# Second layer's first product from seven half-size products, with the first layer's side work on a written-out plan

## The chip, the cores and the metric

One core of a Trainium2 chip runs the whole program. The metric is the device time in microseconds (us) of one execution; lower is better. TensorE multiplies, VectorE (DVE), ScalarE (ACT) and GpSimd (POOL) do everything elementwise, and SyncE (SP) issues nearly all DMAs.

## The reference

```python
def _attn_ref(q, k, v):            # 4 x 8 heads, 576 tokens, 64 wide, float32
    ...
    scores = scale * np.matmul(q_rot, k_rot.transpose(0, 1, 3, 2))
    attn = softmax(scores)
    return np.matmul(attn, v)

def _moe_ref(x, w_in, w_out):      # first layer: x 2304 x 512, w_in 512 x 2048, w_out 2048 x 512
    h = np.maximum(x @ w_in, 0.0)
    return h * h @ w_out

def _moe2_ref(x, w_in, w_out, alpha):   # second layer, same sizes
    h = x @ w_in
    g = np.maximum(h, 0.0) + alpha * np.minimum(h, 0.0)
    return g @ w_out
```

Attention, then the first layer on its output, then the second layer. The weights arrive as float64 and are converted on the chip.

## The kernel before

**Precision.** Every float32 operand of the two layers is split into a high part, rounded to the format that TensorE takes at full rate, and a low part, the rest. A product is three matmuls: high by high, high by low, low by high. So every operand needs a copy to the high part (ACT) and a subtraction for the low part (DVE).

**Units.** The 2304 tokens are NB = 6 blocks of W = 384. A *unit* (layer, b, z, i) is one step of TensorE: with z = 0 it makes rows i of the hidden layer for block b (12 matmuls of 128 x 384: four parts of the 512-long sum, three matmuls each), with z = 1 it adds hidden rows i to the block's output (12 matmuls of 128 x 384 in the first layer, 9 of 128 x 512 in the second). There are 16 of each per block. Blocks 0 and 1 of the first layer are interleaved and overlap with the end of attention; from block 2 on the order is block by block, 16 units of z = 0 and then 16 of z = 1. `products` issues a unit's matmuls.

**What goes around a unit.** PE, DVE, ACT and POOL run in exactly the order in which the code is written (a manual schedule); SP's order is set by a planner. At step t, after the matmuls of unit t, the code issues `low_g` for unit t + 2 (the low part `gl` of a hidden tile, on DVE), `high_g` for unit t + 3 (the high part `gh`, on ACT), `finish` for unit t - 1, and then the *jobs* of step t. `finish` of a z = 0 unit takes the sum out of PSUM: in the first layer a Relu on ACT (L575) and a square, on ACT for even i (L581) and on POOL for odd i (L583); in the second a Relu on ACT, alpha times the negative part on DVE (L578) and their sum on POOL (L579).

**Jobs.** While the first layer's blocks 2 to 5 run, the second layer's 32 weight tiles (128 x 512 each) are loaded and converted, one every EVERY2 = 2.9 steps. One conversion is a load (three steps ahead), L384, L385 (`convert`) and L390 (`mask`) on DVE, L394 (`grow`) on ACT, L399 and L400 (`sign`) on DVE, then L405 on ACT and L406 on DVE (`join`), and a DMA that keeps the result in HBM. Other jobs prepare the next block's x: a product on POOL (L510, first layer only), the high part on ACT (L520) and the low part on DVE (L526). During the first layer's last block, `hold` loads each kept weight tile into the slot that the first layer has just stopped using.

Of the kernel before, what the change touches and what calls it, by code (L numbers as in the profile page):

```python
# [22 lines left out]
P = 128  # L23
# [328 lines left out]
EVERY0, EVERY1, EVERY2 = 1.8, 1.8, 2.9  # L352


class Weights:
# [55 lines left out]
def moe(tc, xd, rd, mats, pbias, dram, al, out):  # L411
# [11 lines left out]
    with ExitStack() as mo:  # L423
# [4 lines left out]
        Xf = X.rearrange("p y c w -> p (y c w)")  # L428
        Xw = [Xf[:, 1024 * k:1024 * k + 1024].rearrange("p (y n) -> p y n", y=2) for k in range(6)]
# [7 lines left out]
        units += [(layer, b, z, i) for layer in range(2) for b in range(0 if layer else FIRST, NB)  # L437
                  for z in range(2) for i in range(FC)]
# [4 lines left out]
        def slot(z, i):  # L443
            if z and OUT0 <= i < OUT0 + OUTX:
                return Xw[4 + i - OUT0]
            return late[("held0" if i < HELD0 else "held1") if z == 0 else ("out0" if i < OUT0 else "out1")].tile([P, 2, 512], F32R, name="w")

        def place(layer, z, i):
            if layer == 0:
                ws[0, z, i] = slot(z, i)  # L450
                return ws[0, z, i]
            return Xw[3]

        def done_with(wc, *j):
            if j[0]:
# [5 lines left out]
        def hold(z, i):  # L461
            w = slot(z, i)
            nc.sync.dma_start(out=w.bitcast(F32), in_=kept[1, z, i])
            ws[1, z, i] = w
# [4 lines left out]
        def hidden(layer, b, i):  # L469

            if first(layer, b):
# [5 lines left out]
            return gt[k][:, c0:c0 + W]  # L477

# [16 lines left out]
        def load_x(layer, b, c):  # L495
            c0 = b * W
            k = next(xbuf)
            xr, r = XT[:, k, 0], XT[:, k, 1]
            if layer == 0:
                nc.sync.dma_start(out=xr, in_=xd[:, c, c0:c0 + W])  # L500
                for j in range(2):
                    nc.sync.dma_start(out=r[64 * j:64 * j + 64], in_=rd[c, j:j + 1, c0:c0 + W].to_broadcast([D, W]))
            else:
                nc.sync.dma_start(out=xr, in_=x2[:, c, c0:c0 + W])
            xin[layer, b, c] = xr, r
# [22 lines left out]
        def products(u):  # L528
            layer, b, z, i = units[u]
            wh, wl = ws[layer, z, i][:, 0], ws[layer, z, i][:, 1]  # L530
# [9 lines left out]
            if i == 0:  # L540
                accs[layer, b] = [ps_h.tile([P, 512], F32, name="ph") if (layer, b) == (0, FIRST - 1) else
                                  late["ps_y"].tile([P, 512], F32, name=f"py{e}") for e in range(KC if layer == 0 else W // P)]
# [25 lines left out]
        def finish(u):  # L568

            layer, b, z, i = units[u]  # L570
            c0 = b * W
            if z == 0:
# [3 lines left out]
                if layer == 1:  # L576
                    mn = XT[:, u % 2, 1]
                    V.tensor_scalar(mn, ph, 0.0, al[:, i:i + 1], ALU.min, ALU.mult)  # L578
                    G.tensor_tensor(out=g, in0=g, in1=mn, op=ALU.add)  # L579
                elif i % 2 == 0 or first(layer, b):  # L580
                    A.activation(out=g, in_=g, func=AF.Square)  # L581
                else:
                    G.tensor_tensor(out=g, in0=g, in1=g, op=ALU.mult)  # L583
# [39 lines left out]
        for k in range(2 * FC):  # L623
            job(NF + EVERY2 * k, conv[1], 1, k // FC, k % FC)
        for c in range(KC):
            for layer in range(2):
                for b in range(0 if layer else FIRST, NB):
                    prior = (layer, b - 1) if b else (layer - 1, NB - 1)
                    job((NF - 16 if prior == (0, FIRST - 1) else at_unit[prior + (1, 0)]) + 4 * c,
                        ((-2, load_x), (0, join_x), (2, high_x), (3, low_x)), layer, b, c)  # L630
# [13 lines left out]
        late["held0"] = pool("held0", HELD0, side="right")  # L644
# [6 lines left out]
        for t in range(-STEPS_AHEAD - 1, NU + 1):  # L651
            if t == EARLY:
                late.update(held1=pool("held1", FC - HELD0), sp=pool("sp", 3), out0=pool("out0", OUT0),
                            g0=pool("g0", FC // 2), ps_y=pool("ps_y", 1, space=PSUM))
                gfirst = mo.enter_context(ExitStack())
                late["g1"] = gfirst.enter_context(tc.tile_pool(name="g1", bufs=FC // 2))
            if 0 <= t < NU:
                products(t)
# [3 lines left out]
            unfinished += [t - 1] if 0 <= t - 1 < NU else []  # L662
            if "g0" in late:
                while unfinished:
                    finish(unfinished.pop(0))
            if t == at_unit[0, FIRST - 1, 1, FC // 2 - 1]:
                gfirst.close()
                late["out1"] = pool("out1", FC - OUT0 - OUTX)
            for d, stage, j in sorted(jobs.get(t, []), key=lambda x: x[0]):
                stage(*j)  # L670
            if 0 <= t < NU:
                layer, b, z, i = units[t]
                if (layer, b) == (0, NB - 1):
                    hold(z, i)
            if t < EARLY:
                yield
# [56 lines left out]
```

## Time and profile before

| | |
|---|---|
| median of 3 runs | 1131.28 us (1129.35 to 1135.73) |
| the profiled execution | 1133.05 us, of which the span of instructions is 1131.3 us |
| TensorE busy | 1088.7 us (96%), 6480 matmuls |
| DVE, ACT, POOL busy | 600.3, 535.6, 312.3 us |
| mean granted TensorE clock | 0.989 of full speed (2.4 GHz) |
| HBM read and written | 80.26 MB and 31.01 MB |
| first layer, block 2 on | about 463 to 729.5 us |
| second layer | 729.5 us to the end |

Busy shares are means over stages with different limits: attention (to about 330 us), the first layer's blocks 0 and 1 (to about 463 us), its blocks 2 to 5, and the second layer. A matmul's own duration overlaps with the next one's, so the pace of TensorE is read from the distance between starts.

### The profile page before, as it was taken

The page shows a single profiled execution, that of the slowest core. Times are in us where ns is not written, and L with a number is a line of the kernel's source. Part 1 is how long each engine was busy: PE and PEld are TensorE (multiplying, and loading weights), DVE is VectorE, ACT ScalarE, POOL GpSimd, SP SyncE. Part 2 cuts the span into 40 slices and gives each one's busy share as a digit, 9 for nine tenths or more (in the row PEclk, how much of TensorE's full clock was granted, in tenths as well). Part 3 has the DMA queues.
Part 4 walks back from the last instruction along what each step waited for, and adds up shares of the span by engine and source line. Part 5 has one row for each costly group of instructions (what it writes and reads, how often), then busy time and mean ns, then how long its engine had stood idle before and what let it go on. Part 6 is the DMA issues. An engine that isn't in the chain of part 4 may idle for free.

```text
span 1131.3 us, 17531 instructions
## 1 busy us (share of the span) xinstructions
PE 1088.7 (96%) x6480; PEld 996.4 (88%) x6480; DVE 600.3 (53%) x1070; ACT 535.6 (47%) x1140; POOL 312.3 (28%) x304
## 2 busy tenths in 40 slices
PE   2899999999879999999999999999999999999997
PEld 1788887887769999999999999998989989898996
DVE  4665766766568989578596821233232323323232
ACT  1676776776548845455655533232232323223221
POOL 3665446663400000120211201050322305032230
PEclk9999999999979999999999999999999999999999
DMA  7768677675634433557566557800001020000101
GB/s 190 171 172 208 162 180 163 172 192 155 188 94 147 132 111 115 186 173 246 178 210 222 176 192 257 281 2 24 33 14 43 8 49 1 25 33 14 28 1 29
DMA packets 91733, 140.73 MB, mean 124 GB/s; under 512 B 21120, under 2 KB 62720, under 8 KB 91648
## 3 DMA queue, kind: packets, MB, share of 16 engines
q1 hardware_dynamic: 87856, 133.24, 41.1%
q10 hardware_dynamic: 3536, 6.24, 1.7%
q8 instruction: 51, 0.84, 0.3%
q14 instruction: 34, 0.28, 0.1%
q0 software_dynamic: 256, 0.13, 0.0%
HBM read 80.26 MB, written 31.01 MB: 98 GB/s over the span
## 4 chain that ended last, share of the span: by engine, by line
PE 87%; DMA 4%; DVE 3%; SPq 3%; ACT 1%; issue 1%; POOL 0%; ACTq 0%; DVEq 0%; POOLq 0%
PE py L553 32%; PE ph L535 12%; PE ph L536 12%; PE ph L537 12%; PE ps L264 7%; PE sc L196 6%; PE ps L218 4%; PE ph L553 2%; DMA vraw<-in_v_dram 2%; SPq L170 2%; PE ps L149 1%; DMA xt<-r 1%; DVE nm L199 1%; DMA kL<-nat 1%; PE ps L230 1%
## 5 line engine op out<-in xcount | busy, mean ns | idle before, releaser
L535 PE MATMUL ph<-xs,w 128*128 128x384 f32 x768 | 258.2, 336 | 3.2 <-ACT g L575 3.2
L536 PE MATMUL ph<-xs,w 128*128 128x384 f32 x768 | 257.7, 336 | 0.0
L537 PE MATMUL ph<-xs,w 128*128 128x384 f32 x768 | 257.5, 335 | 0.0
L490 DVE TENSOR_TENSOR gl<-g,gh 128x384 fp32r<-128x384 f32 x192 | 109.9, 574 | 174.9 <-PE py L553 123.1
L575 ACT ACTIVATE g<-ph 128x384 f32<-128x384 f32 x192 | 94.4, 492 | 210.0 <-PE ph L537 201.0
L579 POOL TENSOR_TENSOR g<-g,xt 128x384 f32<-128x384 f32 x96 | 101.9, 1062 | 295.5 <-DVE xt L578 295.5
L483 ACT ACTIVATE gh<-g 128x384 fp32r<-128x384 f32 x192 | 100.5, 524 | 160.6 <-PE py L553 145.2
L553 PE MATMUL py<-w,gh 128*128 128x512 f32 x504 | 155.3, 389 | 0.0
L199 DVE TENSOR_REDUCE nm<-sc 128x1 f32<-128x576 f32 x144 | 108.0, 750 | 84.2 <-PE sc L196 83.6
L535 PEld LDWEIGHTS ph<-xs,w 128*128 128x128 f32 x768 | 145.1, 189 | 4.6 <-ACT g L575 3.5
L553 PE MATMUL py<-gh,w 128*128 128x384 f32 x560 | 146.2, 335 | 0.0
L536 PEld LDWEIGHTS ph<-xs,w 128*128 128x128 f32 x768 | 145.1, 189 | 0.2
L537 PEld LDWEIGHTS ph<-xs,w 128*128 128x128 f32 x768 | 145.1, 189 | 0.0
L578 DVE TENSOR_SCALAR xt<-ph,al 128x384 f32<-128x384 f32 x96 | 59.3, 618 | 138.8 <-ACT g L575 132.2
L200 ACT ACTIVATE p<-sc,nm 128x576 f32<-128x576 f32 x144 | 107.0, 743 | 45.3 <-DVE nm L199 36.2
L553 PEld LDWEIGHTS py<-w,gh 128*128 128x128 f32 x504 | 94.5, 188 | 19.4
L553 PEld LDWEIGHTS py<-gh,w 128*128 128x128 f32 x560 | 101.8, 188 | 0.0
L553 PE MATMUL py<-w,gl 128*128 128x512 f32 x252 | 98.2, 389 | 0.0
L553 PE MATMUL py<-gl,w 128*128 128x384 f32 x280 | 94.0, 336 | 1.8 <-DVE gl L490 1.8
L196 PE MATMUL sc<-kH,qT 128*128 128x288 f32 x336 | 82.2, 331 | 12.6 <-DMA qT<-nat 11.3
L218 PE MATMUL ps<-ident,p 128*128 128x128 f32 x576 | 87.1, 279 | 0.2
L510 POOL TENSOR_TENSOR xt<-xt 128x384 f32<-128x384 f32 x24 | 27.5, 1149 | 216.6 <-DMA xt<-x 172.5
(102 smaller groups left out, 1617.7 us busy)
## 6 DMA issues: line engine op xcount, KB each, us to landing
w<-in_moe_w_in_dram SPq DMA_DIRECT2D x32, 512.0 KB
w<-in_moe_w_out_dram SPq DMA_DIRECT2D x32, 512.0 KB
wk<-xs SPq DMA_DIRECT2D x32, 512.0 KB
w<-wk SPq DMA_DIRECT2D x30, 512.0 KB
xt<-x SPq DMA_DIRECT2D x48, 192.0 KB
kH<-nat SPq DMA_DIRECT2D x62, 144.0 KB
qT<-nat SPq DMA_DIRECT2D x62, 144.0 KB
kL<-nat SPq DMA_DIRECT2D x62, 144.0 KB
```

The lines of the kernel that those rows point to most:

```text
L196: T.matmul(sc[:, hf, o0:o0 + w], lhsT=lhs, rhs=kx[:, c0:c0 + w], start=st and y == 0, stop=not st and y == len(prods) - 1 and o0 + w == SH)
L199: V.tensor_reduce(out=nm, in_=sc[:, :, 0:SH], axis=AX.XY, op=ALU.max, negate=True)
L200: A.activation(out=Pt[n, i][:, j * S:(j + 1) * S].rearrange("p (a b) -> p a b", a=2), in_=sc[:, :, 0:SH], func=AF.Exp, bias=nm, accum_out= ...
L218: T.transpose(u[:, c * P:(c + 1) * P], p[:, (S + 64) * j + c * P:(S + 64) * j + (c + 1) * P], ident)
L483: A.activation(out=hi, in_=hidden(layer, b, i), func=AF.Copy)
L490: V.tensor_tensor(out=lo, in0=hidden(layer, b, i), in1=gsp[u][0].bitcast(F32), op=ALU.subtract)
L535: T.matmul(ph[:, :W], lhsT=wh[:, cs], rhs=xh, start=(c == 0), stop=False)
L536: T.matmul(ph[:, :W], lhsT=wh[:, cs], rhs=xl, start=False, stop=False)
L537: T.matmul(ph[:, :W], lhsT=wl[:, cs], rhs=xh, start=False, stop=(c == KC - 1))
L553: T.matmul(acc, lhsT=x, rhs=y, start=(s0 and k == 0), stop=(s1 and k == 2))
L575: A.activation(out=g, in_=ph, func=AF.Relu)
L579: G.tensor_tensor(out=g, in0=g, in1=mn, op=ALU.add)
```

## The change

**Seven products instead of eight.** In the second layer the first product is made for two blocks at once. Weights and x are cut into halves (256 of 512 along the sum, hidden rows i and i + 8, and the two blocks), and the four half products of each pair come from seven products of sums and differences (Strassen's algorithm in Winograd's form). A unit is now (1, 2q, 0, i) for i = 0 to 7: seven products of 6 matmuls of 128 x 384, in the function `seven`. It is followed by the 32 z = 1 units of both blocks.

**What a unit of seven needs.** The x terms (7 per half, `T`, prepared by `prepare` during the z = 1 units before) stay in SBUF. The seven weight pieces of each i (256 KB each, `ws`) lie in HBM and pass through a ring of RING = 8 slots: after each product `refill` issues a DMA for the product eight later. Three PSUM banks A, B and C hold the products; what is in A or B must be copied out (`keep`, ACT) or added into a result (DVE) before the next product accumulates onto that bank. `leak` (DVE) and `join` (ACT, POOL) make the four hidden tiles.

**The first layer.** The weight pieces are made there: for each i, `sums` adds and subtracts the two converted halves: ten operations on POOL (two of 512 columns, eight of 256) with four copies on ACT between them, over six steps. Conversions stand at the steps in `TURNS` instead of every 2.9 steps, with the stages one step closer together, and use two load buffers of `st[0]` instead of four. All squares are on ACT.

```diff
-EVERY0, EVERY1, EVERY2 = 1.8, 1.8, 2.9
+EVERY0, EVERY1 = 1.8, 1.8
+SUMS_AT = 0, 0, 1, 2, 2, 2, 3, 3, 3, 4, 4, 4, 5, 5
+TURNS = {2: ((0, "in"), (3, "in"), (6, "out"), (10, "in"), (13, "in"), (16, "out"), (19, "out"), (21, "out"), (24, "in"), (27, "in")),
+         3: ((3, "in"), (6, "in"), (9, "out"), (12, "out"), (18, "out"), (21, "out"), (24, "in"), (27, "in")),
...
+RING = 8
+PRODUCTS = (0, "A", "11"), (1, "C", "21"), (2, "A", "T2"), (3, "B", "T1"), (4, "A", "T3"), (5, "B", "22"), (6, "A", "T4")
...
-                       ((-3, self.load), (0, self.convert), (1, self.mask), (2, self.grow), (3, self.sign), (4, self.join)))
+                       ((-3, self.load), (0, self.convert), (0, self.mask), (1, self.grow), (2, self.sign), (3, self.join)))
...
-        w64 = st[n // 2 % 2].tile([P, 512, 2], U32, name="w64", bufs=2)
+        w64 = st[0 if layer else n // 2 % 2].tile([P, 512, 2], U32, name="w64", bufs=2)
...
+        def sums(i, x):
+            u, v = (t.bitcast(F32) for t in late["pair"])
...
+            if x < 2:
+                t = (u, v)[x]
+                G.tensor_tensor(out=t[:, 0], in0=t[:, 0], in1=t[:, 1], op=ALU.add)
+                return
...
+            if x == 0:
+                G.tensor_tensor(out=f[k], in0=a, in1=b, op=op)
+            elif x == 1:
+                A.activation(out=o[:, 0], in_=f[k], func=AF.Copy)
+            else:
+                G.tensor_tensor(out=o[:, 1], in0=f[k], in1=o[:, 0].bitcast(F32), op=ALU.subtract)
+                nc.sync.dma_start(out=kept[i][:, p], in_=o.bitcast(F32))
...
+        def refill(n):
+            if n < 7 * HC * NG:
+                w = late["ring"][n % RING]
+                nc.sync.dma_start(out=w.bitcast(F32), in_=kept[n // 7 % HC][:, n % 7])
...
+        def seven(u):
...
+            def leak(n, ph):
+                s[n] = low()
+                V.tensor_scalar(s[n], ph, 0.0, al[:, i + HC * (n // 2):i + HC * (n // 2) + 1], ALU.min, ALU.mult)
+
+            def join(n, ph):
+                A.activation(out=h[n], in_=ph, func=AF.Relu)
+                G.tensor_tensor(out=h[n], in0=h[n], in1=s[n], op=ALU.add)
+
+            def keep(x, c):
+                s[x] = part()
+                A.activation(out=s[x], in_=bank[c], func=AF.Copy)
+
+            for p, c, x in PRODUCTS:
...
+                refill(k + p + RING)
+                if p == 0:
+                    keep("1", "A")
+                    if late.get("rest"):
+                        late.pop("rest")()
+                elif p == 1:
+                    V.tensor_tensor(out=h[0], in0=bank["C"], in1=s["1"], op=ALU.add)
+                    leak(0, h[0])
+                elif p == 2:
+                    keep("2", "A")
+                    join(0, h[0])
+                elif p == 3:
+                    keep("5", "B")
+                elif p == 4:
+                    V.tensor_tensor(out=h[3], in0=bank["A"], in1=s["5"], op=ALU.add)
+                    leak(3, h[3])
+                elif p == 5:
+                    V.tensor_tensor(out=h[1], in0=bank["B"], in1=s["2"], op=ALU.add)
+                    leak(1, h[1])
+                    join(3, h[3])
...
-                if layer == 1:
-                    mn = XT[:, u % 2, 1]
-                    V.tensor_scalar(mn, ph, 0.0, al[:, i:i + 1], ALU.min, ALU.mult)
-                    G.tensor_tensor(out=g, in0=g, in1=mn, op=ALU.add)
-                elif i % 2 == 0 or first(layer, b):
-                    A.activation(out=g, in_=g, func=AF.Square)
-                else:
-                    G.tensor_tensor(out=g, in0=g, in1=g, op=ALU.mult)
+                A.activation(out=g, in_=g, func=AF.Square)
...
-        for k in range(2 * FC):
-            job(NF + EVERY2 * k, conv[1], 1, k // FC, k % FC)
+                if z == 0 and i >= HC:
+                    for x, n in enumerate(SUMS_AT):
+                        job(at + 4 + n, ((0, sums),), i - HC, x)
```

POOL's order in the first layer, block 2 on, before: products of x (L510) and squares (L583) of the four blocks, nothing else.

```order
L510 TENSOR_TENSOR xt<-xt 128x384 x4
L583 TENSOR_TENSOR g<-g 128x384 x8
L510 TENSOR_TENSOR xt<-xt 128x384 x4
L583 TENSOR_TENSOR g<-g 128x384 x8
L510 TENSOR_TENSOR xt<-xt 128x384 x4
```

After, POOL's piece that falls into block 2's z = 1 units (`w_5594` and `w_5595` are the two converted halves, `q` a spare tile; L657 is the product of x, before L510):

```order
L657 TENSOR_TENSOR xt<-xt 128x384
L494 TENSOR_TENSOR w_5594<-w_5594 128x512
L494 TENSOR_TENSOR w_5595<-w_5595 128x512
L501 TENSOR_TENSOR w_5594<-w_5595 128x256
L505 TENSOR_TENSOR w_5595<-w_5594,w_5595 128x256
L501 TENSOR_TENSOR w_5594<-w_5594 128x256
L505 TENSOR_TENSOR q<-w_5594,q 128x256
L501 TENSOR_TENSOR w_5594<-w_5594,w_5595 128x256
L657 TENSOR_TENSOR xt<-xt 128x384
L505 TENSOR_TENSOR w_5595<-w_5594,w_5595 128x256
L501 TENSOR_TENSOR w_5594<-w_5594 128x256
L505 TENSOR_TENSOR q<-w_5594,q 128x256
```

Squares have left POOL; ten operations of the sums now lie between the products of x, in z = 1 units. DVE's order in the same units after the change (L640 is `gl`, before L490; L673 the low part of x; L393, L394, L399, L408, L409 and L415 are a conversion's L384, L385, L390, L399, L400 and L406 of before):

```order
L393 TENSOR_SCALAR m<-w_5896 128x512
L394 SCALAR_TENSOR_TENSOR m<-w_5896,m 128x512
L399 TENSOR_SCALAR w_5896<-w_5896 128x512
L640 TENSOR_TENSOR gl<-g,gh 128x384 x2
L408 SCALAR_TENSOR_TENSOR w_5896<-w_5896 128x512
L409 TENSOR_SCALAR w_5896<-w_5896 128x512
L393 TENSOR_SCALAR m<-w_5940 128x512
L394 SCALAR_TENSOR_TENSOR m<-w_5940,m 128x512
L399 TENSOR_SCALAR w_5940<-w_5940 128x512
L640 TENSOR_TENSOR gl<-g,gh 128x384
L415 SCALAR_TENSOR_TENSOR xs<-m,w_5896 128x512
L640 TENSOR_TENSOR gl<-g,gh 128x384
```

Conversions at steps 19 and 21 follow each other with two steps between, and TensorE's `gl` tiles stand behind them in the queue.

TensorE's order in one unit of seven after the first (`ph` are the PSUM banks, `xs` the ring), with what each row waits for:

```order
L599 MATMUL ph<-T,xs 128x384 [waits DMAHW3_49]
L599 MATMUL ph<-T,xs 128x384 x5
L599 MATMUL ph<-T,xs 128x384 [waits DMAHW4_49]
L599 MATMUL ph<-T,xs 128x384 x5
L599 MATMUL ph<-T,xs 128x384 [waits DMAHW5_49,Activation_49]
L599 MATMUL ph<-T,xs 128x384 x5
L599 MATMUL ph<-T,xs 128x384 [waits DMAHW6_49,DVE_49]
L599 MATMUL ph<-T,xs 128x384 x5
L599 MATMUL ph<-T,xs 128x384 [waits DMAHW7_49,Activation_49]
L599 MATMUL ph<-T,xs 128x384 x5
L599 MATMUL ph<-T,xs 128x384 [waits DMAHW0_49,Activation_49]
L599 MATMUL ph<-T,xs 128x384 x5
```

The seventh product (again 6 matmuls) waits for a DMA and DVE. A unit of z = 0 had 12 matmuls and one wait for a bank that had been free for three units; now every product of 6 waits for its refill, and the third to the seventh also for an engine that empties a bank.

## Rows read from the trace of the kernel before

**Rows 1.** Page, section 1: busy time, share of the span, instructions.
```profile
PE 1088.7 (96%) x6480; PEld 996.4 (88%) x6480; DVE 600.3 (53%) x1070; ACT 535.6 (47%) x1140; POOL 312.3 (28%) x304
```

**Rows 2.** Windows: stretch, length, busy us of each engine, clock, DMA share, GB/s.
```profile
430.00:463.00 33.00, 31.23 (x171) 30.89 (x170) 27.77 (x51) 15.45 (x30) 2.53 (x2) 0.95 0.50 162
496.50:529.80 33.30, 33.30 (x194) 33.30 (x193) 28.08 (x51) 16.80 (x31) 5.69 (x5) 1.00 0.67 218
696.20:729.50 33.30, 33.30 (x194) 33.30 (x193) 9.69 (x18) 9.45 (x19) 0.83 (x1) 1.00 0.86 272
729.50:762.80 33.30, 33.30 (x193) 33.30 (x193) 11.22 (x19) 9.04 (x19) 15.45 (x15) 1.00 0.16 53
```

**Rows 3.** Chain that ended last, in order of time: start us, us, what.
```profile
40.83 2.90 DMA kL<-nat
...
449.05 3.01 PE py L553 x11
452.07 2.86 PE ph L553 x12
...
563.09 33.28 PE py L553 x192
```

**Rows 4.** Timeline at a unit's end: start us, us, engine, line, operation.
```profile
731.41 0.33 PE L535 MATMUL ph<-xs,w 128*128 128x384 f32 x1
...
731.61 0.49 ACT L575 ACTIVATE g<-ph 128x384 f32<-128x384 f32 x1 [2.11 <-PE ph L537]
```

**Rows 5.** Timeline where TensorE waits for a bank to be emptied.
```profile
331.39 0.48 ACT L575 ACTIVATE g<-ph 128x384 f32<-128x384 f32 x1
...
331.92 0.29 PEld L535 LDWEIGHTS ph<-xs,w 128*128 128x128 f32 x1 [3.55 <-ACT g L575]
```

**Rows 6.** Lines by form, whole span: count, busy us, mean ns, idle before.
```profile
L579 POOL TENSOR_TENSOR g<-g,xt 128x384 f32<-128x384 f32 x96 | 101.9, 1062 | 295.5 <-DVE xt L578 295.5
L575 ACT ACTIVATE g<-ph 128x384 f32<-128x384 f32 x192 | 94.4, 492 | 210.0 <-PE ph L537 201.0 <-issue 8.6
L124 POOL TENSOR_TENSOR t<-kraw,tab 128x640 f32<-128x640 f32 x15 | 23.4, 1558 | 108.4 <-DMA kraw<-in_k_dram 86.0 <-DVE nm L199 14.3 <-DMA al<-in_moe_alpha_dram 7.5
L141 DVE TENSOR_TENSOR nat<-ps,nat 128x512 fp32r<-128x512 f32 x32 | 22.0, 687 | 2.0 <-ACT nat L140 1.8
L125 POOL TENSOR_TENSOR t<-kraw,tab 128x320 f32<-128x320 f32 x15 | 13.1, 872 | 0.0
L141 DVE TENSOR_TENSOR nat<-ps,nat 128x256 fp32r<-128x256 f32 x16 | 6.6, 415 | 0.0
```

**Rows 7.** Lines on DVE from 395 to 430 us, while POOL is idle.
```profile
L490 DVE TENSOR_TENSOR gl<-g,gh 128x384 fp32r<-128x384 f32 x16 | 8.8, 554 | 5.5 <-PE ph L553 3.0 <-PE py L553 2.5
L385 DVE SCALAR_TENSOR_TENSOR m<-w,m 128x512 f32<-128x512 uint32 x7 | 4.9, 694 | 0.2
L399 DVE SCALAR_TENSOR_TENSOR w<-w 128x512 uint32<-128x512 uint32 x6 | 4.1, 685 | 0.0
L390 DVE TENSOR_SCALAR w<-w 128x512 uint32<-128x512 uint32 x7 | 3.0, 430 | 0.2
L384 DVE TENSOR_SCALAR m<-w 128x512 uint32<-128x512 uint32 x7 | 3.0, 422 | 0.1
L406 DVE SCALAR_TENSOR_TENSOR w<-m,w 128x512 fp32r<-128x512 f32 x4 | 2.8, 694 | 0.1
L400 DVE TENSOR_SCALAR w<-w 128x512 uint32<-128x512 uint32 x6 | 2.6, 431 | 0.2
```

**Rows 8.** Timelines where DVE and POOL work at the same time.
```profile
99.77 0.69 DVE L141 TENSOR_TENSOR nat<-ps,nat 128x512 fp32r<-128x512 f32 x1
99.86 0.88 POOL L125 TENSOR_TENSOR t<-kraw,tab 128x320 f32<-128x320 f32 x1
...
507.87 1.55 POOL L510 TENSOR_TENSOR xt<-xt 128x384 f32<-128x384 f32 x1 [7.64 <-DMA xt<-x]
...
508.46 1.25 DVE L390 TENSOR_SCALAR w<-w 128x512 uint32<-128x512 uint32 x1
```

More of the change, by code (lines that the diff above doesn't have):

```diff
@@ L451, in place @@
                 return ws[0, z, i]
-            return Xw[3]
+            if z:
+                return Xw[3]
+            if "pair" not in late:
+                late["pair"] = [st[1].tile([P, 512, 2], U32, name="w64", bufs=2).rearrange("p n t -> p (n t)").bitcast(F32R)
+                                .rearrange("p (y n) -> p y n", y=2) for _ in range(2)]
+            return late["pair"][i // HC]
         def done_with(wc, *j):
-            if j[0]:
+            layer, z, i = j
+            if layer and z:
@@ L456, in done_with @@
                 kept[j] = dram.tile([P, 2, 512], F32, name="wk%d_%d_%d" % j)
                 nc.sync.dma_start(out=kept[j], in_=wc.bitcast(F32))
-        weights = Weights(tc, mats, pbias, place, done_with)
[L461 to L464, printed above, removed]
+            elif layer and i < HC:
+                kept[i] = dram.tile([P, 7, 2, 256], F32, name=f"ws{i}")
+                for k in range(2):
+                    nc.sync.dma_start(out=kept[i][:, k], in_=wc[:, :, 256 * k:256 * k + 256].bitcast(F32))
+            elif layer:
+                nc.sync.dma_start(out=kept[i - HC][:, 6], in_=wc[:, :, 256:512].bitcast(F32))
@@ L466, in first, with hold @@
+        def hold(i):
+            w = slot(1, i)
+            nc.sync.dma_start(out=w.bitcast(F32), in_=kept[1, 1, i])
+            ws[1, 1, i] = w
         def first(layer, b):
@@ new lines, in seven, with rest @@
+        def seven(u):
+            layer, b, z, i = units[u]
+            if "banks" not in late:
+                late["full"] = [ps_h.tile([P, 512], F32, name="ph") for _ in range(4)]
+                late["banks"] = [t[:, :W] for t in late["full"]]
+            bank = dict(zip("ABC", (late["banks"][i % 2], late["banks"][2], late["banks"][3])))
+            g = late["g0"].tile([P, XW], F32, name="g")
+            gt[i], gt[i + HC] = (g[:, :W], g[:, W:]), late["more"][2 * i:2 * i + 2]
+            h = [*gt[i], *gt[i + HC]]
+            part, low = (lambda x=x: next(late[x]) for x in ("part", "leak"))
+            k = 7 * (b // 2 * HC + i)
+            s = {}
+            def leak(n, ph):
[8 more added lines that the diff above has]
+            for p, c, x in PRODUCTS:
+                w = late["ring"][(k + p) % RING]
+                for kc in range(2):
+                    ws_, t = slice(128 * kc, 128 * kc + 128), late["T"][x, kc]
+                    first_ = p in (0, 1, 3)
+                    for n, (y0, y1) in enumerate(((0, 0), (0, 1), (1, 0))):
+                        T.matmul(bank[c], lhsT=w[:, y0, ws_], rhs=t[:, y1], start=first_ and kc == 0 and n == 0,
+                                 stop=kc == 1 and n == 2, skip_group_check=not first_)
+                refill(k + p + RING)
[18 more added lines that the diff above has]
+                    join(3, h[3])
+            def rest():
+                leak(2, bank["A"])
+                join(1, h[1])
+                join(2, bank["A"])
+            late["rest"] = rest
@@ L529, in products @@
             layer, b, z, i = units[u]
+            if layer and z == 0:
+                seven(u)
+                return
+            if late.get("rest"):
+                late.pop("rest")()
             wh, wl = ws[layer, z, i][:, 0], ws[layer, z, i][:, 1]
@@ L541, in products @@
                 accs[layer, b] = [ps_h.tile([P, 512], F32, name="ph") if (layer, b) == (0, FIRST - 1) else
-                                  late["ps_y"].tile([P, 512], F32, name=f"py{e}") for e in range(KC if layer == 0 else W // P)]
+                                  late["full"][1 + e] if layer and b % 2 and e < 2 else
+                                  late["ps_y"].tile([P, 512], F32, name=f"py{3 if layer and b % 2 else e}") for e in range(KC if layer == 0 else W // P)]
             gh, gl = gsp.pop(u)
@@ L571, in finish @@
             c0 = b * W
+            if layer and z == 0:
+                return
             if z == 0:
@@ L657, in moe @@
             if 0 <= t < NU:
+                if units[t][0] and units[t][2:] == (0, 0):
+                    finish(t - 1)
                 products(t)
@@ L661, in moe @@
                     split(t + d)
-            unfinished += [t - 1] if 0 <= t - 1 < NU else []
+            unfinished += [t - 1] if 0 <= t - 1 < NU and not (t < NU and units[t][0] and units[t][2:] == (0, 0)) else []
             if "g0" in late:
```

100 lines of the change are left out of this document (82 added, 18 removed).

## The prediction

> **What bounds the kernel now.** I read the page's busy times first: TensorE works 1088.7 of 1131.3 us [rows 1]. Then the windows by stage: from block 2 of the first layer to the end TensorE is busy for the whole of each stretch at full clock, while DVE, ACT and POOL have room [rows 2]. So after 463 us the time is TensorE's, and what the change gives or takes is read in its pace. One set of 16 units with 384-column matmuls takes 33.28 us for 192 of them [rows 3]: 173.3 ns a matmul, 2.08 us a unit. The second layer's z = 0 sets have that same length (729.5 to 762.8 us) [rows 2].
>
> The third view is the chain, where it leaves TensorE. The last such place is at 449 us: DVE is late with a `gl`, and TensorE's next 11 matmuls take 3.01 us and the next 12 take 2.86, where 1.91 and 2.08 are due [rows 3]. In 430 to 463 us TensorE is busy 31.23 of 33.00, DVE is at 27.77, and the granted clock averages 0.95 [rows 2]. A wait of 1.8 us thus cost about 1.8 us once more, at the lower clock level. A loaded DVE is what this kernel must fear.
>
> **What the seven products save.** Before: 6 blocks x 33.28 = 199.7 us. After: 3 pairs x 8 units x 42 matmuls x 0.1733 = 174.7 us. Columns, type and weight loads per matmul are as before, so I take the same pace. Term: **-25.0 us**, if TensorE never waits.
>
> **Hand-offs inside a unit of seven.** Each product lasts 6 x 0.1733 = 1.04 us. What it left in bank A or B must be out before the product after next begins, so the cover is one product. ACT starts 0.20 us after the first matmul of the next unit starts [rows 4] and takes 0.492 [rows 6]; TensorE goes on 0.05 us after ACT's end (331.39 + 0.48 to 331.92) [rows 5]. `keep` is thus through after 0.74 us, 0.30 before it is needed. The addition of `h[3]` on DVE reads one operand from PSUM and one from SBUF; the trace has 0.415 us for 256 columns and 0.687 for 512 [rows 6], so 0.55 for 384, and 0.80 in all: 0.24 to spare, less the 0.17 by which a weight load runs ahead. ACT's seven operations take some 3.5 us of a unit's 7.28, DVE's three additions and four leaks about 4, POOL's four additions 4 x 1.06 = 4.2 [rows 6]: all fit. I allow 0.06 us a unit: **+1.5 us**. Bounds: 0; and, if POOL stretched the addition of `h[3]` as it stretched L390 (0.43 to 1.25) [rows 7, 8], 0.5 us a unit, +12. I stay near zero, because the operation with the same kinds of operands ran 0.69 us under a POOL operation [rows 8], the 0.687 of its mean.
>
> **The first layer.** Here TensorE has no slack, so the change can only cost. ACT gains eight squares of about 0.5 us and some short copies per block of 66 us, and was about half busy (16.8 of 33.3 us in block 2's z = 1 set) [rows 2]. What counts is DVE and POOL together. L390 started while POOL's L510 ran and took 1.25 us instead of 0.43; it ended 0.29 us after L510, which itself took 1.55 [rows 7, 8] where 384 columns mean 1.06 [rows 6]. SBUF-to-SBUF work of the two runs one after the other. The Trainium skill (GPSIMD Engine Reference, "Specifications") says that GpSimd's SBUF interfaces are shared with VectorE, with contention for DVE operations in a 2-port mode or with two SBUF inputs. By that rule, which names no price, the extra POOL work costs something wherever such operations meet; by the row it is the full length of the operation, and my sum goes by the row.
>
> So I add up both engines' work in block 2's units 16 to 24 (z = 1), where TURNS starts conversions at steps 16, 19, 21 and 24 and `sums` lies on steps 17 to 22. A conversion's six DVE operations take 3.36 us: 1.55 at its step, 1.12 two steps on, 0.69 three steps on [rows 7]. In these nine steps stand four firsts, three seconds and four thirds: 12.3 us. Nine `gl` and two low parts of x at 0.554 [rows 7] add 6.1. POOL: by the line through 0.872 for 320 columns and 1.558 for 640 [rows 6] an operation of 256 takes 0.74 and one of 512 takes 1.28, so `sums` is 8.5 us; three products of x at 1.0 add 3. Together 29.9 us, in 9 x 2.08 = 18.7: 11.2 us behind. The same nine units before, with conversions at 17, 20 and 23, hold 10.1 + 6.1 + 3 = 19.2, no more than fits, and TensorE did not wait there [rows 2].
>
> The slack is that `gl` is issued two units ahead: 4.16 us, plus 0.17 (it enters with the second matmul), less 0.55 and 0.05: 3.7 us. Behind DVE in its queue stand the next `gl`; TensorE waits for those. If everything stood in one line the lag over the slack would be 7.5 us. It ends lower if POOL's operations fall behind rather than DVE's; in that case DVE alone (18.4 us in 18.7) is never late. The two alternate in rows 8, so I take about half, 4 us of waiting, and 2 us for the lower clock, by the 449 us place. Term: **+6 us**; bounds 0 and +11 (7.5 and half again). By the same count no other stretch of blocks 2 to 5 lags over 3 us, since there the sums lie in z = 0 units, where DVE owes TensorE nothing but a few operations. SP's stores change from 32 of 512 KB to 16 of those and 56 pieces of 256 KB, 16.8 to 23.1 MB over four blocks; with a DMA share of 0.67 [rows 2] I take them as hidden.
>
> **The step into the second layer.** During the first layer's last 16 units SP issues the 16 `hold` loads (8.4 MB), 8 refills (2.1) and x in four pieces (1.6): 12.1 MB in 33.3 us. Before, 272 GB/s stood at a DMA share of 0.86 [rows 2], so 316 at full share, and 12.1 MB need 38 us. ACT's high parts of the second x half stand ahead of `gh` in its queue, with three units of slack. I take **+1 us**, bounds 0 and +5.
>
> **Sum.** -25.0 + 1.5 + 6 + 1 = -16.5: the span goes from 1131.3 to 1114.8 us. The profiled execution took 1133.05 us, 1.75 around its span, and lies 1.8 above the median of 1131.28; the median should thus come to **1115 us**.
>
> **The rivals.**
>
> *No overload* (24 in 100): POOL's sums slip behind and DVE keeps its pace. For it: POOL has no deadline in those steps. Against: rows 8. Time: 1131.3 - 25 + 2.5 = 1109 us.
>
> *Hand-offs show* (10): DVE's addition of `h[3]` or ACT's `keep` comes 0.5 us late in each unit. For it: the spare time is 0.1 to 0.3 us. Against: the operands' kinds in rows 8. Time: 1115 + 10.5 = 1125 us.
>
> *The overload recurs* (8): ACT stands behind the sums' copies in blocks 3 to 5 too, and Relu or `gh` come late, say 4 us at each of three places. For it: the copies wait for POOL within ACT's queue. Against: four PSUM banks give three units of slack. Time: 1127 us.
>
> *The ring starves* (5), the slower side: a product needs 256 KB in 1.04 us, 252 GB/s over 58 us, three times. Rows 2 have 272 GB/s at 0.86 share, with 512 KB transfers. The gain is gone where a product takes 66.56 / 56 = 1.19 us, that is, below 220 GB/s; at 200 GB/s it takes 1.31, 168 products cost 45 us more, and the kernel ends near 1159 us. The chain waits 2.90 us for a transfer of 144 KB [rows 3]; with fewer than 2.5 in flight the ring starves, with the eight that the slots allow it does not. The Trainium skill (DMA: Bandwidth & Descriptors, "Measured (HBM→SBUF, 128 partitions, SWDGE, issued from GpSimd)") advises batches of 1 MiB or more and fits 2.0 us plus bytes over 436 GB/s for one transfer: an estimate of 2.6 us for a refill, some 100 GB/s if they ran one by one. No row here has them one by one.
>
> **How the numbers follow.** My forecast's own case (1110 to 1121 us) has 46 in 100; 7 are left for what I don't see. About 0.5% (5.7 us) is what a measurement of this kernel can tell from no change. Faster (below 1125.6): the forecast, no overload, half of the hand-offs and of the recurrence, some of the rest: 0.82. The same: the other halves: 0.10. Slower: the ring and the unseen: 0.08. The range, 1106 to 1127 us, starts at all costs nil (1106.3) and takes in all but the ring and part of the two cases above 1125.
>
> **What would show it.** Seven units: 56 products in 58 to 60 us, TensorE's idle time before L599 near zero; if hand-offs show, waits for DVE L615 or ACT L591 before L599. First layer: block 2's z = 1 set about 39 us instead of 33.3, with TensorE waiting for DVE L640 and the clock below 1.00; the other sets 33.3. DVE operations next to POOL's L494, L501 and L505 twice their length or more. I am wrong if block 2 is 33.3 us long, if waits recur in blocks 3 to 5, or if L599 waits for DMA.

## The result and the profile after

The changed kernel takes 1118.80 us (median of 4 runs, 1116.98 to 1121.38); the kernel before took 1130.32 beside it (1128.69 to 1135.73). The ratio is 0.9892, 95% interval 0.9851 to 0.9932: some 1.1% faster. The prediction was 1115 us, range 1106 to 1127. The profiled execution took 1117.80 us with a span of 1116.0, 15.3 less than before's; -16.5 had been forecast. The medians lie only 11.5 us apart; executions of one kernel differ by 4 to 7 us here.

TensorE's line in the first section of the page, against [rows 1]:

```profile
PE 1065.8 (96%) x6336; PEld 971.4 (87%) x6336; DVE 682.8 (61%) x1160; ACT 598.4 (54%) x1294; POOL 392.1 (35%) x376
```

The windows of the changed kernel, against [rows 2]: block 2's z = 0 set, its z = 1 set, block 5's z = 1 set (the step into the second layer), and the first stretch of 56 products. Columns: stretch, length, busy us and instructions of PE, PEld, DVE, ACT and POOL, granted clock, DMA share, GB/s.

```profile
461.68:494.96 33.28, 33.28 (x193) 33.28 (x193) 19.96 (x31) 22.28 (x46) 10.16 (x11) 1.00 0.48 161
494.96:535.35 40.39, 34.71 (x193) 33.14 (x193) 34.49 (x52) 18.84 (x39) 15.67 (x14) 1.00 0.65 208
701.75:739.04 37.29, 35.39 (x194) 34.82 (x193) 19.01 (x28) 14.79 (x33) 10.59 (x10) 0.95 0.94 329
739.04:797.56 58.52, 58.52 (x338) 58.38 (x337) 29.35 (x57) 26.11 (x58) 31.34 (x30) 1.00 0.89 283
```

Two of these sets are longer than 33.28 us, and in both TensorE's busy time falls short of the length. In the first, DVE's 34.49 us of work in a set that should last 33.28 say at once which engine to ask about. The longer pieces of the changed kernel's chain from there on (start us, us, what):

```profile
494.00 5.03 DMA w<-in_moe_w_out_dram
500.59 2.65 DVE gl L640 x2
...
511.83 1.40 DVE m L394
...
516.19 5.13 DMA wk<-xs
...
568.63 33.28 PE py L706 x192
635.19 33.28 PE py L706 x192
701.75 4.00 PE py L706 x23
707.81 6.93 DMA w<-x
715.34 1.20 DVE gl L640
716.58 22.47 PE py L706 x119
739.04 58.52 PE ph L599 x336
...
862.89 58.42 PE ph L599 x336
...
986.63 58.40 PE ph L599 x336
```

Three readings. The seven products take 58.52, 58.42 and 58.40 us, and TensorE waits for nothing in them. In block 2's z = 1 set the chain runs beside TensorE from 494.0 to 524.8 us: through DVE operations of up to 1.65 us, twice their usual length and more, as forecast, but also through two transfers of 5 us, a load of weights and the store of a converted tile, which the prediction had at nothing. At the step into the second layer a transfer of 6.93 us stands in the chain, the load of x. TensorE waits 1.9 us there; the rest of that set's 4.0 us is a lower granted clock (0.95): soon after the waits eleven matmuls start 0.27 to 0.32 us apart instead of 0.173.

The waits of the changed kernel in block 2's z = 1 set (engine, line, for whom: us, times, longest):

```profile
PE py L706 <- DVE gl L640: 5.7, 4, 2.9
ACT xs L414 <- DMA wk<-xs: 5.4, 1, 5.4
...
DVE xs L415 <- DMA wk<-xs: 1.9, 1, 1.9
```

The other 1.4 us by which this set is longer are no lower clock, which is 1.00 there. They stand at the edges of the waits: a matmul that is due 0.173 us after the last one's start is counted as waiting only from the last one's end, 0.16 us later, and the one behind it follows after 0.28 us.

Set by set, in the profiled executions:

| piece | before | after | difference | predicted |
|---|---|---|---|---|
| up to block 2 | 463.25 | 461.68 | -1.6 | 0 |
| block 2, z = 1 | 33.28 | 40.39 | +7.1 | +6 (0 to 11) |
| block 5, z = 1 | 33.28 | 37.29 | +4.0 | +1 (0 to 5) |
| other sets of blocks 2 to 5 | 33.28 each | 33.28 each | 0 | 0 |
| first products of layer two | 199.8 | 175.3 | -24.5 | -25.0 + 1.5 |
| the rest | | | -0.3 | 0 |

The first row can't be told from chance: in the eleven runs below, whose kernels hardly differ up to there, block 2 starts between 459.1 and 465.8 us. Sets are therefore compared one by one, not spans.

### The profile page after: what moved, and what is told of

Read it like the earlier page. It is cut to its first block, busy times and chain, and to the rows that moved or that the text cites. A ratio compares the mean times of both kernels' runs of the same rounds, so it can differ in the third digit from the quotient of the medians.

```text
span 1116.0 us, 18143 instructions
## 1 busy us (share of the span) xinstructions
PE 1065.8 (96%) x6336; PEld 971.4 (87%) x6336; DVE 682.8 (61%) x1160; ACT 598.4 (54%) x1294; POOL 392.1 (35%) x376
## 4 chain that ended last, share of the span: by engine, by line
PE 81%; DMA 7%; DVE 5%; SPq 3%; ACT 1%; issue 1%; POOL 1%; DVEq 0%; ACTq 0%; POOLq 0%
PE py L706 24%; PE ph L599 16%; PE ph L706 8%; PE ps L264 7%; PE sc L196 6%; PE ph L687 5%; PE ph L688 5%; PE ph L689 5%; PE ps L218 4%; DMA vraw<-in_v_dram 3%; SPq L170 2%; DVE gl L640 1%; DVE nm L199 1%; PE ps L149 1%; DVE m L394 1%
## 5 line engine op out<-in xcount | busy, mean ns | idle before, releaser
L640 DVE TENSOR_TENSOR gl<-g,gh 128x384 fp32r<-128x384 f32 x189 | 130.5, 695 | 126.3 <-PE py L706 109.2
L599 PE MATMUL ph<-T,xs 128*128 128x384 f32 x1008 | 175.8, 335 | 0.0
L599 PEld LDWEIGHTS ph<-T,xs 128*128 128x128 f32 x1008 | 175.3, 188 | 0.3
L687 PE MATMUL ph<-xs,held 128*128 128x384 f32 x384 | 129.2, 336 | 3.5 <-ACT g L730 3.5
L688 PE MATMUL ph<-xs,held 128*128 128x384 f32 x384 | 129.0, 336 | 0.0
L689 PE MATMUL ph<-xs,held 128*128 128x384 f32 x384 | 128.9, 336 | 0.0
L706 PE MATMUL py<-w,gh 128*128 128x512 f32 x336 | 103.5, 389 | 0.0
L657 POOL TENSOR_TENSOR xt<-xt 128x384 f32<-128x384 f32 x24 | 27.3, 1141 | 202.3 <-DMA xt<-x 168.5
L587 POOL TENSOR_TENSOR g<-g,m 128x384 f32<-128x384 f32 x62 | 67.5, 1096 | 73.2 <-ACT g L586 72.9
L687 PEld LDWEIGHTS ph<-xs,held 128*128 128x128 f32 x384 | 72.5, 189 | 4.3 <-ACT g L730 3.8
L196 PE MATMUL sc<-kL,qT 128*128 128x288 f32 x336 | 72.0, 300 | 3.5 <-DMA kL<-nat 3.5
L706 PEld LDWEIGHTS py<-w,gh 128*128 128x128 f32 x336 | 63.0, 188 | 13.0
L218 PEld LDWEIGHTS ps<-ident,p 128*128 128x128 f32 x576 | 66.7, 141 | 8.8 <-ACT p L200 5.7
L196 PEld LDWEIGHTS sc<-kH,qT 128*128 128x128 f32 x336 | 52.3, 195 | 24.8 <-issue 15.7
```

The lines of the kernel that those rows point to most:

```text
L196: T.matmul(sc[:, hf, o0:o0 + w], lhsT=lhs, rhs=kx[:, c0:c0 + w], start=st and y == 0, stop=not st and y == len(prods) - 1 and o0 + w == SH)
L218: T.transpose(u[:, c * P:(c + 1) * P], p[:, (S + 64) * j + c * P:(S + 64) * j + (c + 1) * P], ident)
L599: T.matmul(bank[c], lhsT=w[:, y0, ws_], rhs=t[:, y1], start=first_ and kc == 0 and n == 0, stop=kc == 1 and n == 2, skip_group_check=not f ...
L640: V.tensor_tensor(out=lo, in0=hidden(layer, b, i), in1=gsp[u][0].bitcast(F32), op=ALU.subtract)
L687: T.matmul(ph[:, :W], lhsT=wh[:, cs], rhs=xh, start=(c == 0), stop=False)
L688: T.matmul(ph[:, :W], lhsT=wh[:, cs], rhs=xl, start=False, stop=False)
```

## The experiments

The two losses were each given two theories. For block 2: **A**, SBUF-to-SBUF work of DVE and POOL in one line, against **B**, transfers made late by conversions two steps apart. For the step: **C**, x stands behind the ring's refills in SP's queue, against **D**, too many bytes in one set. What came out (waiting is TensorE's for `gl` in block 2's set; a set at a clock below 1.00 is longer by that too; lines of kernels with added code are shifted by 1 to 3):

| run | block 2, z = 1 | waiting | clock there | block 5, z = 1 | time, median (runs) |
|---|---|---|---|---|---|
| changed kernel | 40.39 | 5.7 | 1.00 | 37.29 | 1118.80 (4) |
| e1_even | 38.41 | 3.0 | 0.96 | 37.16 | 1115.90 (4) |
| e1b_even | 38.54 | 4.1 | 1.00 | 37.16 | 1119.90 (1) |
| e2_nosums | 37.62 | 2.7 | 0.95 | 37.63 | 1118.29 (1) |
| e2b_nosums | 38.87 | 3.4 | 0.96 | 36.39 | 1113.03 (1) |
| e12_both | 33.28 | 0 | 1.00 | 36.04 | 1110.91 (1) |
| e3_xfirst | 40.05 | 5.6 | 1.00 | 33.28 | 1117.68 (4) |
| e3b_xfirst | 42.97 | 5.8 | 0.92 | 33.28 | 1118.31 (4) |
| e4_squares | 40.34 | 5.9 | 1.00 | 39.12 | 1123.75 (10) |
| e5_ring4 | 39.82 | 5.1 | 1.00 | 33.30 | 1140.44 (1) |
| e7b_one | 34.74 | 0.9 | 1.00 | 33.28 | 1109.42 (4) |
| e7_best | 33.28 | 0 | 1.00 | 33.28 | 1105.05 (6) |

**Even steps for block 2's conversions** (twice).

```diff
-(16, "out"), (19, "out"), (21, "out"), (24, "in"), (27, "in")),
+(16, "out"), (19, "out"), (22, "out"), (25, "in"), (28, "in")),
```

> Block 2's last conversions start at steps 16, 19, 22, 25 and 28 instead of 16, 19, 21, 24 and 27; every sum stays where it was. Theory A (SBUF-to-SBUF work of VectorE and GpSimd runs one after the other, and the sums on steps 17 to 22 push the `gl` back): the amount of work in steps 16 to 24 falls only by one first part, so block 2's z = 1 set stays at 38 to 41 us (40.4 in the changed kernel). Theory B (two conversions two steps apart meet in the one slot from which they are stored and in the two load buffers, and a transfer of about 5 us stands in the path): three steps are 6.2 us, the transfers are through, and the set takes 33.3 to 35 us, the kernel 5 to 7 us less than the changed one. Both in part: 35 to 38 us.

> The plan with even steps (16, 19, 22, 25, 28) once more, because block 2's z = 1 set took 39.8 to 43.0 us in five kernels that leave its plan alone, and one look at 38.4 us doesn't stand clear of that. If even steps take a part of the loss away: 37.5 to 39.3 us. If the first look was chance: 40 us or more.

Measured: 38.41 and 38.54 us, where the five runs that leave this set's plan alone (changed, e3, e3b, e4, e5) have 39.8 to 43.0; TensorE waits 3.0 and 4.1 us, there 5.1 to 5.9. In neither run does an engine still wait for the store, for which ACT had waited 5.4 us and DVE 1.9. So a small part goes away, and B alone is not the cause. The chain of the first of the two runs in that set (its longer pieces: start us, us, what) has one weight load at its start, and from then on DVE alone, up to TensorE's last wait:

```profile
492.52 4.70 DMA w<-in_moe_w_out_dram
498.78 2.12 DVE gl L640 x2
...
510.13 1.42 DVE xs L415
...
514.49 1.36 DVE gl L640
515.89 16.25 PE py L706 x83
```

In the second run the chain goes through POOL's sums, a store of them, and one weight load of 6.19 us that SP issues right after that store. So what even steps leave is not everywhere DVE alone: POOL is late too, and what SP issues behind its stores.

**Without GpSimd's operations for the second pair** (twice). Line of code, three times alike:

```diff
-                G.tensor_tensor(out=f[k], in0=a, in1=b, op=op)
+                if i != 1:
+                    G.tensor_tensor(out=f[k], in0=a, in1=b, op=op)
```

> Leaves out GpSimd's ten operations for the sums of the second pair of weight halves (the one whose sums lie on block 2's steps 17 to 22); ScalarE's copies and the stores of these tiles stay, the plan of the conversions too. Theory A: without GpSimd's work VectorE keeps its pace and block 2's z = 1 set takes 33.3 to 35 us. Theory B: the two conversions two steps apart still wait for their slot and buffers: 38 to 40.4 us.

> The kernel without GpSimd's ten operations for the second pair once more, for the same reason (first look 37.6 us). If these operations bring a part of the loss and the transfers the rest: 37 to 39 us, VectorE busy about 29 us for the same 52 operations that took 34.5 with them. If chance: 40 us or more.

Measured: 37.62 and 38.87 us. So A alone is not the cause either. DVE does keep its pace now: lines of DVE in block 2's z = 1 set, of the changed kernel and then of this one (count, busy us, mean ns, idle before):

```profile
L640 DVE TENSOR_TENSOR gl<-g,gh 128x384 fp32r<-128x384 f32 x14 | 10.1, 743 | 0.0
L394 DVE SCALAR_TENSOR_TENSOR m<-w,m 128x512 f32<-128x512 uint32 x5 | 4.2, 832 | 0.2
...
L399 DVE TENSOR_SCALAR w<-w 128x512 uint32<-128x512 uint32 x5 | 3.2, 645 | 0.2
L393 DVE TENSOR_SCALAR m<-w 128x512 uint32<-128x512 uint32 x5 | 3.2, 635 | 2.2 <-DMA w<-in_moe_w_out_dram 2.2
```

```profile
L643 DVE TENSOR_TENSOR gl<-g,gh 128x384 fp32r<-128x384 f32 x14 | 7.5, 551 | 0.7 <-PE py L709 0.5
...
L394 DVE SCALAR_TENSOR_TENSOR m<-w,m 128x512 f32<-128x512 uint32 x5 | 3.5, 693 | 0.2
L399 DVE TENSOR_SCALAR w<-w 128x512 uint32<-128x512 uint32 x5 | 2.8, 563 | 0.2
...
L393 DVE TENSOR_SCALAR m<-w 128x512 uint32<-128x512 uint32 x5 | 2.1, 424 | 2.2 <-DMA w<-in_moe_w_out_dram 2.2
```

The same 52 DVE operations take 28.9 us instead of 34.5, and `gl` (551 ns), L394 (693) and L393 (424) are back at the means of [rows 7]. L399's mean of 563 is four operations of 0.43 us and one of 1.10, which starts while POOL works on a product of x that this kernel still has. POOL's busy time falls from 15.67 to 4.59 us, so 11.1 us of its work had cost DVE 5.6. Which of the two pays shows in the timelines of the changed kernel (start us, us, engine, line, operation; two pieces, each of DVE and POOL):

```profile
513.88 0.79 POOL L501 TENSOR_TENSOR w<-w 128x256 f32<-128x256 f32 x1
514.01 1.08 DVE L640 TENSOR_TENSOR gl<-g,gh 128x384 fp32r<-128x384 f32 x1
...
522.48 0.69 DVE L394 SCALAR_TENSOR_TENSOR m<-w,m 128x512 f32<-128x512 uint32 x1
522.58 1.45 POOL L657 TENSOR_TENSOR xt<-xt 128x384 f32<-128x384 f32 x1 [5.00 <-DMA xt<-r]
523.21 1.10 DVE L399 TENSOR_SCALAR w<-w 128x512 uint32<-128x512 uint32 x1
```

L394 starts before POOL's operation and takes its usual 0.69 us; `gl` and L399 start during one, and end 0.42 and 0.28 us after it. In this set all thirteen DVE operations that start while POOL works take 2 to 3.3 times their usual length, and the seven that POOL joins later take no more than usual. The Trainium skill (GPSIMD Engine Reference, "Specifications") states contention between the two engines for DVE operations with two SBUF inputs or in a 2-port mode, without a price. For `gl` and L394, which have two such inputs, these rows agree; L393 and L399 have one, and no row shows their mode.

Leaving POOL's operations out also takes away what waits for them: in the changed kernel's set SP waits 3.8 us for a sum before it issues its store, and ACT 1.5 us before a copy. How much of the gain is that was not taken apart. What holds the set up now is in the waits of this kernel in this set (engine, line, for whom: us, times, longest):

```profile
ACT xs L414 <- DMA wk<-xs: 4.0, 1, 4.0
...
DVE xs L415 <- DMA wk<-xs: 2.8, 1, 2.8
...
PE py L709 <- DVE gl L643: 2.7, 1, 2.7
```

The conversion of step 21 may not write its two halves (ACT L414, DVE L415) before the store of the one from step 19 has left `Xw[3]`. Behind L414 in ACT's queue stand the next `gh`, behind L415 the next `gl`, and TensorE waits 2.7 us for that `gl`. In the second run the same store takes 5.95 us in the chain, and TensorE waits 3.4.

**Both together.** The two edits in one kernel.

> The even steps of the first experiment and the left out GpSimd operations of the second together. Theories A and B both say 33.3 us for block 2's z = 1 set, at a granted clock of 1.00. More than 34 us would mean that neither is the cause.

Measured: 33.28 us at a clock of 1.00, TensorE busy throughout:

```profile
496.41:529.69 33.28, 33.28 (x193) 33.28 (x193) 28.72 (x52) 19.29 (x38) 3.86 (x3) 1.00 0.73 237
```

So A and B are both causes (the two edits together ran once), and either by itself leaves 4.3 to 5.6 us of a loss of about 7; in three of the four runs with one edit the clock was 0.95 or 0.96, which is 1.5 to 1.9 us of that. The parts don't add up; that a DVE late for one reason hides the lateness from the other would explain it, and was not shown.

**The x load ahead of the refills** (twice).

```diff
+            prepare(0, 0, "load")
             for n in range(RING):
                 refill(n)
...
-                job(u, ((0, prepare),), q, kc, "load")
+                if q or kc:
+                    job(u, ((0, prepare),), q, kc, "load")
```

> The first load of x for the second layer is issued ahead of seven of the ring's eight first refills instead of behind all eight. Theory C (block 5's z = 1 set takes 37.3 us because this load stands behind the refills in the queue, and T's parts come late on ScalarE and VectorE, ahead of `gh` and `gl`): the set takes 33.3 to 34.5 us and the kernel 3 to 4 us less than the changed one. Theory D (some 12 MB in one set are more than the transfers give, so that something is late in any order, then a weight tile of the last block): 36 to 38 us, TensorE waiting at its output product for a transfer of w. Block 2's set stays at 40.4 us.

> The same kernel as the one with the x load ahead of the refills, once more, because its four times lay between 1111 and 1121 us and only the fastest was profiled. Theory C: block 5's z = 1 set is 33.3 to 34.5 us again, and what differs between executions lies elsewhere (the set of block 2, or the step at the end of block 1). The other: the set at the step is 36 us or more this time, and the early load is not a cure but luck.

Measured: block 5's z = 1 set is 33.28 us in both runs, as C says, and in both later kernels with the edit (one refill of the eight still goes ahead of the load). SP's timeline, of the changed kernel (its set starts at 701.75) and of this one (699.12): start us, us, engine, line, operation.

```profile
703.93 3.36 SPq L548 DMA_DIRECT2D xs<-ws  x7
707.34 1.20 SPq L558 DMA_DIRECT2D w<-x  x2
```

```profile
701.26 0.92 SPq L559 DMA_DIRECT2D w<-x  x2
702.23 3.56 SPq L549 DMA_DIRECT2D xs<-ws  x7
```

The load is issued 5.6 us into the set before, 2.1 us into it now. D falls by its window, where the same bytes go through at 366 GB/s, a DMA share of 0.98, and TensorE waits for nothing:

```profile
699.12:732.40 33.28, 33.28 (x193) 33.28 (x193) 19.66 (x28) 15.14 (x33) 10.93 (x10) 1.00 0.98 366
```

The median falls only by 0.5 to 1.1 us against the changed kernel's, less than its four times spread (1111 to 1121). The two profiled executions, 1109.4 and 1117.5 us of span, differ by 4.3 up to block 2, 2.9 in block 2's set (a clock of 1.00 against 0.92) and 0.9 in the first 56 products. The 4 us are thus shown by the set, in both executions, not by the median of this kernel.

**The squares back on GpSimd.** In `finish`, for layer one, with an odd `i` from block 2 on:

```diff
-                A.activation(out=g, in_=g, func=AF.Square)
+                if i % 2 == 0 or first(layer, b):
+                    A.activation(out=g, in_=g, func=AF.Square)
+                else:
+                    G.tensor_tensor(out=g, in0=g, in1=g, op=ALU.mult)
```

> One part of the change undone: the square of every odd unit of blocks 2 to 5 is GpSimd's again, as before the change. Theory E (the squares don't matter: TensorE waits for nothing in a z = 0 set, and GpSimd has room there): the z = 0 sets stay at 33.3 us, VectorE's busy time in them grows because SBUF-to-SBUF work of the two engines stands in line (about 20 us in block 2's set now, 24 or more then), block 2's z = 1 set stays within 1 us of 40.4, the kernel within 2 us of the changed one. Theory F (moving the squares is what lets the sums fit beside the conversions): eight operations of about 1 us on GpSimd push the sums and the conversions later in the z = 0 sets, the z = 1 sets of blocks 3 and 4 then grow beyond 33.3 us, or block 2's by 2 us and more, and the kernel is 3 to 10 us slower than the changed one.

Measured: 1123.75 us, ratio to before 0.9940 (0.9918 to 0.9962), where the changed kernel has 0.9892. E is right about blocks 2 to 4, whose sets stay as they were, but not about the kernel's time; F is right about the size, but not about the place. The windows of block 5, z = 0 and z = 1:

```profile
671.31:704.59 33.28, 33.28 (x193) 33.28 (x193) 28.07 (x33) 19.86 (x43) 23.36 (x24) 1.00 0.53 185
704.59:743.71 39.12, 35.21 (x193) 34.63 (x193) 20.86 (x30) 15.15 (x33) 13.19 (x12) 0.96 0.89 310
```

POOL has 23.4 us of work in the z = 0 set instead of 16.7, in its queue the sums stand behind squares that wait for ACT, and the last sum ends 3.2 us into the next set instead of 1.8. Its store and the x load come later in SP's queue, x at 712.06, 7.5 us into the set. So all squares on ScalarE are worth some 2 us at this step, and the rest of the 5 us (the first stretch of products at 59.84 us, executions that differ) was not taken apart.

**Four slots in the ring.** `RING = 4` for `RING = 8`, so that half as many refills are under way.

> Four slots in the ring instead of eight, so that a refill has 3.1 us before TensorE needs it instead of 7.3. As the prediction reckoned (starving starts below 2.5 in flight, from 2.90 us for one transfer): 58.4 to 61 us for each of the three stretches of 56 products. The rival: a refill beside the others takes longer than 3.1 us from issue to landing (a wait on one of 5.9 us stood in the chain of the even-step run): at 5.5 us four slots give four products in 6.5 us, so 75 to 92 us for each stretch, with TensorE waiting for the transfers from ws, and a kernel of 1165 to 1215 us. Block 5's z = 1 set has four refills less ahead of its x load: by theory C 34 to 36 us instead of 37.3.

Measured: stretches of 70.64, 68.80 and 65.21 us and 1140.44 us in all: slower than before the change, between the two forecasts. The chain of its first stretch (its first longer pieces):

```profile
732.38 1.98 PE ph L599 x12
734.36 5.86 DMA xs<-ws
740.36 7.03 PE ph L599 x24
747.40 3.41 DMA xs<-ws
```

Refills that TensorE waits for take 3.2 to 5.9 us here, longer than the 3.1 us that four slots give and less than the 7.3 of eight. The 2.90 us from which the prediction judged the ring [rows 3] were too short. The Trainium skill (DMA: Bandwidth & Descriptors, "Anatomy of one DMA — SWDGE (gpsimd) path") fits 2.0 us plus the bytes over 436 GB/s to one transfer issued by GpSimd: an estimate of 2.6 us for a refill. SP issues these, and no refill runs alone here. This kernel's block 5 set, with four refills less ahead of x, is 33.30 us, which speaks for C once more.

**The repairs together.** Two plans, both with the x load ahead. The smaller one, which ran after the other, moves one conversion out of block 2's z = 1 set and sets those left 4, 4 and 3 steps apart:

```diff
-TURNS = {2: ((0, "in"), (3, "in"), (6, "out"), (10, "in"), (13, "in"), (16, "out"), (19, "out"), (21, "out"), (24, "in"), (27, "in")),
-         3: ((3, "in"), ...
+TURNS = {2: ((0, "in"), (3, "in"), (6, "out"), (10, "in"), (13, "in"), (16, "out"), (20, "out"), (24, "in"), (27, "in")),
+         3: ((0, "out"), (3, "in"), ...
```

> The x load ahead of the refills, and of the two-part plan only the second part: the sums of the second pair stay on steps 17 to 22, one conversion is moved from block 2's z = 1 set to step 0 of block 3, and those left start at steps 16, 20, 24 and 27. By the prediction's count the nine units 16 to 24 then hold 9.0 us of conversions, 6.1 of other VectorE work and 11.5 of GpSimd's, 26.6 where 18.7 fit: 7.9 us behind against a slack of 3.7, half of the rest as waiting and some clock, 35 to 36.5 us for the set. If it is the transfers that decide once the work fits in VectorE's own queue: 33.3 to 34.3 us, and a kernel within 2 us of the two-part plan's 1105.

Measured: 34.74 us for the set, 1109.42 us, ratio 0.9815 (0.9782 to 0.9847). The set lies between the forecasts. TensorE waits once, 0.9 us, and the chain into that wait is DVE beside the sums, so the work still does not quite fit; the prediction's count made more of it (1.7 to 3.2 us over 33.28, against 1.5). The larger plan also starts the six conversions before step 19 three units earlier, among them the first two pairs of halves, so that their sums move too:

```diff
+TURNS = {2: ((-3, "in"), (0, "in"), (3, "out"), (7, "in"), (10, "in"), (13, "out"), (19, "out"), (24, "in"), (27, "in")),
```

> Both repairs at once: the x load ahead of the refills, and a plan for blocks 2 and 3 in which the first four conversions start three units earlier (steps -3, 0, 7 and 10), so that the second pair's sums lie on steps 14 to 19, one conversion that stores from the shared slot is moved from block 2's set z = 1 to step 0 of block 3, and no two start less than three steps apart. Theories A and B with C: block 2's z = 1 set 33.3 to 34.5 us, block 5's 33.3 to 34.5 us, the seven products as they are, so 7 + 4 us less than the changed kernel's span of 1116.0: a kernel of 1105 to 1109 us. The rival: the step at the end of block 1, where VectorE is already late, takes the three units' work badly, or the transfers vary from run to run: 1110 to 1118 us.

Measured: 1105.05 us (1103.44 to 1108.84), ratio 0.9786 (0.9757 to 0.9815). Its chain has the z = 1 sets of blocks 2 to 5 at 33.28 us, and starts a z = 0 set as long after each, up to the products:

```profile
493.45 33.28 PE py L707 x192
560.01 33.28 PE py L707 x192
626.58 33.28 PE py L707 x192
693.13 33.28 PE py L707 x192
726.41 58.39 PE ph L600 x336
```

Its span is 12.7 us under the changed kernel's: 7.1 in block 2, 4.0 in block 5, 1.5 before block 2, 0.1 in the first products.

## Why the prediction was right, and where it was not

- **Seven products, hand-offs, ring.** Forecast -25.0 and +1.5, together -23.5; measured -24.5. A stretch of 336 matmuls at 173.3 ns is 58.24 us, so the hand-offs cost 0.2 to 0.3 us in each instead of 0.5. The row by which GpSimd was to leave DVE's additions alone could not show it: L141 starts at 99.77 us, 0.09 before POOL's operation [rows 8], and in block 2's set no operation that started first was stretched either. It came true all the same: in the first stretch seven of eight additions of `h[0]` (L607, one operand in PSUM) start while POOL works, and all eight take 0.56 us; those of `h[3]` never start beside POOL there. The ring held with eight slots for the reason given (enough in flight), but the number in flight that it needs was set too low, as the run with four slots shows.
- **Block 2, z = 1.** Forecast +6 for this set and no other, with TensorE waiting for `gl`; measured +7.1, there alone. The size was right, the mechanism only half. Right: DVE and POOL in one line, at 743 ns instead of 551 for a `gl`, and about half of POOL's work falling on DVE (5.6 of 11.1 us). Missing: the sentence that the transfers are hidden looked at SP's stores as a sum of bytes, and not at the one slot and the two load buffers that two conversions two steps apart have to share. That alone cost 4.3 to 5.6 us, with POOL's operations left out; what the prediction had reckoned cost 5.1 and 5.3, with even steps (the second time with a load in the path). Wrong as well was "the clock below 1.00": it was 1.00 in that set, and the 4 us of waiting and 2 of lower clock were 5.7 and 1.4 of slow restarts. That +6 lies so near +7.1 is partly luck, since two causes of 4 to 6 us each came to 7 and not to their sum.
- **The step into the second layer.** The term of +1 is the one that was mis-sized: +4.0, inside its bounds. The reason given there, 38 us for 12.1 MB from an extrapolated 316 GB/s, is wrong: 366 GB/s were reached. What the step overlooked is the place of the x load in SP's queue, behind eight refills. By the prediction's own sign, waits that recur in blocks 3 to 5, this set counts against it.
- **The rivals.** No overload: false for the changed kernel, and what the repaired one comes to (1105 measured, 1109 worked out). The recurrence in blocks 3 to 5: false, these sets take 33.28 us but for the last, whose cause is another. Hand-offs and a starving ring: not at these sizes.
- **The sum.** That -15.3 lies so near -16.5 owes 1.6 us to the stretch before block 2; the two losses together were 11.1 us, not 7.

## What to carry to other kernels

Where side work is put on a plan by hand, two counts are needed for each place and neither replaces the other: the work of engines that stretch each other's operations (here DVE and POOL), and for each buffer the time from one use to the next against the time of the transfer between them (here 2 steps of 2.08 us against a store of 5.1 us). Loads that something soon waits for belong ahead of those that fill a ring for later, since a queue issues them in order. An experiment that takes away one suspected cause and moves little has not cleared it: take both away before either is dismissed.

## What was not expected of the hardware

- Transfers of 256 to 512 KB together ran at 366 GB/s with a DMA share of 0.98 over a whole set, and TensorE kept a clock of 1.00 without a wait.
- Beside GpSimd it was the order of starting that decided who paid: a DVE operation from SBUF to SBUF that began during a POOL operation ended 0.28 to 0.56 us after it (thirteen of thirteen), one that began first kept its usual time (seven of seven).
- The granted clock did not follow the sum of TensorE's waits: with the same code in block 2's z = 1 set, 5.7 us of waiting went with 1.00 (40.39 us) and 5.8 us with 0.92 (42.97 us); with even steps, 4.1 us with 1.00 and 3.0 us with 0.96. What decides it stays open.
